# First-batch changes to a fused attention and maxout kernel: two weights loaded earlier, the v prefetch later, a z copy on ScalarE, more filler matmuls

## The chip, the cores and the metric

The kernel runs on one core of one Trainium2 chip. The metric is the device time of one execution in microseconds (us). Before the change it was 980.92 us, the median of three runs (979.39 to 981.77). All runs quoted here gave a correct result. Engines are named as in the profile: PE is TensorE's matmuls, PEld its weight loads, DVE is VectorE, ACT is ScalarE, POOL is GpSimd, SP is SyncE. POOL issues the software DMA queue here, SP the hardware one with all DMA transposes.

## The reference, cut to what matters

```python
batch, seq, d_model, d_qk = 8, 3072, 256, 64          # u, v: batch x seq x 256; z: batch x seq x 64
scores = (1.0 / S) * np.matmul(z, z.transpose(0, 2, 1))
attn = np.maximum(scores, 0.0) ** 2
x = u * np.matmul(attn, v)                             # then flattened to 24576 x 256
h1 = x @ w1                                            # w1, w2: 256 x 1024
h2 = x @ w2
out = np.maximum(h1, h2) @ w_out                       # w_out: 1024 x 256
```

The scores are symmetric in their two rows of z, and the kernel uses this: it computes a block of squared scores once and gets the mirrored block by a DMA transpose. It also uses max(h1, h2) = relu(h1 - h2) + h2, so it needs w1 - w2, and the product of w2 with w_out.

## The kernel before

A batch has 24 tiles of 128 rows, in 6 groups of 4 tiles. For each group the kernel forms products of all 24 tiles of attention with v in four PSUM accumulators (`attn_unit`), then empties ("drains") them, multiplies by u ("gate") and runs the two dense layers one group later. The first dense layers come after group 2, two groups at once. Everything that follows plays in the first three groups of batch 0, about the first 70 us.

Four parts matter. First, blocks of attention lie in 11 rotating buffers, and mirrors that are needed late are put off into a list:

```python
    apool = ctx.enter_context(tc.tile_pool(name="apool", bufs=11))
    ...
    def score_pair(b, g, m, dve_half=None, halves=False):
        blk = m // 2
        if m % 2 == 0:
            A[b, g, blk] = apool.tile([P, G, GW], bf16, name="a_sb")
        ...                                   # two score matmuls, ReLU of each half on ACT or DVE
        if not halves:
            nc.vector.tensor_mul(a[:, k : k + 2, :], r, r)
        if m % 2 == 1 and blk > g:
            if b == 0 and g < 2 and blk > 2:
                later.append((b, g, blk))
            else:
                mirror(b, g, blk)

    def mirror(b, g, blk):
        t = tpool.tile([P, G, G, P], bf16, name="at_sb")
        nc.sync.dma_start_transpose(...)      # reads A[b, g, blk], 0.5 MB
```

A new block whose buffer is still the source of a mirror must wait until that mirror has landed. Second, the loads of the weights, of the next u, of batch 1's z and of batch 1's v all go down one software queue, in program order:

```python
                if i + 1 < len(groups):
                    if i and n == 1:
                        load_u(*groups[i + 1])          # nc.gpsimd.dma_start
                    if n == 16:
                        turn_u(*groups[i + 1])          # nc.sync.dma_start_transpose
                if i == 1 and n == 6:
                    nc.vector.memset(w2_sb[:, 0, 0:1], 0.0)
                    for w_sb, w in ((w2_sb, moe_w2), (w1_sb, moe_w1), (w_out_sb, moe_w_out)):
                        nc.gpsimd.dma_start(
                            out=w_sb, in_=w.rearrange("(c p) f -> p c f", p=P)
                        )
                if later and n % 4 == 0 and (i > 1 or i == 1 and n > 12):
                    mirror(*later.pop(0))
                ...
                    if g == 2 and n == 10:
                        load_z(b + 1, 0, NT)
                    ...
                    if g >= 3 and n in (8, 14):
                        load_v(b + 1, (2 * (g - 3) + (n == 14)) * G, G)
```

The one-element memset makes the weight loads wait until DVE gets there. Each u has two natural-layout buffers (`unat`, bufs=2), so a load of u waits for the DMA transpose of the u two groups earlier, and what lies behind it in the queue waits too. Third, z is turned on PE at the start and copied out of PSUM by DVE or ACT:

```python
                if i == 0 and n == 5:
                    zT_pe(0, 12, 8, "dve")
                if i == 0 and n == 11:
                    zT_pe(0, 20, 4, "act")
```

Fourth, PE starts on dummy ("filler") matmuls, of which five lie between the first real pieces of work:

```python
        keep_warm([GW] * 5 + [P] * 2)
        ...
        zT_pe(0, 0, 4, "dve")
        keep_warm([P] * 5)
        ...
        ahead(1)
        zT_pe(0, 4, 8, "act")
        ahead(3)
```

`ahead(k)` computes score pairs up to number k. Of the first 22 pairs some have one ReLU half on DVE.

Of the kernel before, what the change touches and what calls it, by code (L numbers as in the profile page):

```python
# [11 lines left out]
def kernel(  # L12
# [10 lines left out]
    nc = tc.nc  # L23
    fp32 = mybir.dt.float32
# [8 lines left out]
    P = 128  # L33
    R = 64
    NT = S // P
    G = 4
    GW = G * P
    NG = NT // G
    KD = D // P
# [56 lines left out]
    def zT_pe(b, lo, n, engine):  # L96
        tp = mm_psum.tile([P, n, P], bf16, name="tpz", tag="mm")
        for j in range(n):
            nc.tensor.transpose(
                tp[:, j, :], zd[b][:, lo + j, :, :].rearrange("p h d -> p (h d)"), ident  # L100
            )
        copy = nc.scalar.copy if engine == "act" else nc.vector.tensor_copy
        copy(zT[b][:, lo : lo + n, :], tp)  # L103
# [18 lines left out]

    A = {}
    later = []

    def score_pair(b, g, m, dve_half=None, halves=False):
        blk = m // 2
# [142 lines left out]
    done = 0  # L270

    def ahead(upto):
        nonlocal done
        while done < min(upto, len(pairs)):
            early = done < 22
            score_pair(
                *pairs[done],
                dve_half=1 if early and (done % 2 == 0 or done < 2) else None,
                halves=done == 0,
            )  # L280
            done += 1
# [6 lines left out]
    with tc.manual_schedule():  # L288
        z32a = first_z(0, 4)
        z32b = first_z(4, 8)  # L290
        z32c = first_z(12, 12)
        warm = consts.tile([P, GW], bf16)
        nc.vector.memset(warm, 0.0)
        load_v(0, 0, G)
        make_identity(nc, ident)
        for g in range(1, NG):
            load_v(0, g * G, G)
        load_u(0, 0)
        load_u(0, 1)
        w1_sb = tpool.tile([P, KD, Dff], bf16, name="w1", tag="at_sb")  # L300
        w2_sb = tpool.tile([P, KD, Dff], bf16, name="w2", tag="at_sb")
        w2T_sb = tpool.tile([P, KD, KF, P], bf16, name="w2T", tag="at_sb")


        w_ps = mm_psum.tile([P, GW], fp32, name="warm_ps", tag="mm")

        def keep_warm(cols):
            for w in cols:
                nc.tensor.matmul(w_ps[:, :w], warm[:, :P], warm[:, :w], start=True, stop=True)

        keep_warm([GW] * 5 + [P] * 2)
        double_first(z32a, 0, 4)
        zT_pe(0, 0, 4, "dve")
        keep_warm([P] * 5)
        double_first(z32b, 4, 4)
        double_first(z32b, 8, 4, at=4)
        on_pool = (nc.gpsimd.tensor_copy, nc.gpsimd.tensor_copy)
        for c in range(0, 12, 4):
            double_first(z32c, 12 + c, 4, at=c, copies=on_pool)
        ahead(1)  # L320
        zT_pe(0, 4, 8, "act")
        ahead(3)

        waiting, sums = [], None
        for i, (b, g) in enumerate(groups):
            acc = [
                acc_psum.tile([P, KD, GW], fp32, name=f"acc{half}") for half in range(2)
            ]
            for n in range(NT):
                k = need[i, n]  # L330
                if b == 0 and g < 2:
                    ahead(max(k, done + 1) if n % 2 == 0 and n < 22 else k)
                else:
                    more = n in (0, 3, 6, 9, 12, 15, 18, 20)
                    ahead(max(k, min(done + 1, k + AHEAD)) if more else k)
                if i == 0 and n == 5:
                    zT_pe(0, 12, 8, "dve")
                if i == 0 and n == 11:
                    zT_pe(0, 20, 4, "act")
                attn_unit(b, g, n, acc, n == 0, n == NT - 1)  # L340
                if i and n == 12:
                    waiting.append((*groups[i - 1], gate(*groups[i - 1], sums)))
                if i == 0 and n == 14:
                    turn_u(0, 0)
                if i + 1 < len(groups):
                    if i and n == 1:
                        load_u(*groups[i + 1])
                    if n == 16:
                        turn_u(*groups[i + 1])
                if i == 1 and n == 6:  # L350

                    nc.vector.memset(w2_sb[:, 0, 0:1], 0.0)
                    for w_sb, w in ((w2_sb, moe_w2), (w1_sb, moe_w1), (w_out_sb, moe_w_out)):
                        nc.gpsimd.dma_start(
                            out=w_sb, in_=w.rearrange("(c p) f -> p c f", p=P)
                        )
                if later and n % 4 == 0 and (i > 1 or i == 1 and n > 12):
                    mirror(*later.pop(0))
                if i == 2 and n == 16:
                    nc.vector.tensor_sub(w15_sb, w1_sb, w2_sb)  # L360
                    for dc in range(KD):
                        tp = mm_psum.tile([P, KF, P], bf16, name="tpw", tag="mm")
                        for j in range(KF):
                            nc.tensor.transpose(
                                tp[:, j, :], w2_sb[:, dc, ts(j, P)], ident
                            )
                        nc.scalar.copy(w2T_sb[:, dc, :, :], tp)
                if b + 1 < B:
                    if g == 2 and n == 10:
                        load_z(b + 1, 0, NT)  # L370
                    if g == 3 and n == 4:
                        double_z(b + 1, 0, NT)
                        zT_dma(b + 1)
                    if g >= 3 and n in (8, 14):
                        load_v(b + 1, (2 * (g - 3) + (n == 14)) * G, G)
            if i == 2:
                for dc in range(KD):
                    ps = mm_psum.tile([P, D], fp32, name="w2o_ps", tag="mm")
                    for nb in range(KF):
                        nc.tensor.matmul(  # L380
                            ps,
                            w2T_sb[:, dc, nb, :],
                            w_out_sb[:, nb, :],
                            start=(nb == 0),
                            stop=(nb == KF - 1),
                        )
                    nc.scalar.copy(W2o_sb[:, dc, :], ps)

            now = waiting if i >= 2 else []
            g_sbs = [ff(w) for w in now[:1]]  # L390
            sums = drain(acc)
            for j, w in enumerate(now):
                if j:
                    g_sbs.append(ff(w))
                ff2(*w, g_sbs[j])
            if now:
                waiting = []
        w = (*groups[-1], gate(*groups[-1], sums))
        ff2(*w, ff(w), last=True)
# [29 lines left out]
```

## Time and profile before

| | value | where it is read |
|---|---|---|
| time, three runs | 980.92 us (979.39 to 981.77) | times |
| the execution that was profiled | 985.42 us, span 983.4 us, mean granted clock 0.996 | times, page |
| PE busy | 967.5 us, 98% of the span | part 1 of the page |
| PE waits for the gate of the dense layer (g_sb) | 4.6 us, once | waits of PE |
| clock from 62 to 66 us | 0.50 | busy time by stretch |

The page of the kernel before gives busy times (part 1) and the shares of the chain that ended last (part 4):

```profile
span 983.4 us, 19128 instructions
...
PE 967.5 (98%) x8036; PEld 517.9 (53%) x8036; DVE 497.4 (51%) x755; ACT 577.9 (59%) x1054; POOL 60.5 (6%) x118
...
PE 95%; DMA 3%; DVE 1%; ACT 0%; SPq 0%; issue 0%; DVEq 0%
```

PE bounds the kernel. The 3% of DMA in the chain is one transfer. The waits of PE in the kernel before (columns: who waited, for whom, total us, times, longest us):

```profile
PE d_ps L214 <- DVE g_sb L224: 4.6, 1, 4.6
PE acc_638 L183 <- DVE h_sb L194: 1.8, 1, 1.8
...
PE s_ps L135 <- DVE zT L103: 1.5, 1, 1.5
...
PE s_ps L135 <- ACT zT L103: 0.8, 1, 0.8
PE s_ps L135 <- DVE r_sb L146: 0.3, 1, 0.3
```

The waits of DVE in the kernel before, from 30 to 70 us, show why g_sb was late: DVE stood in its queue before a squaring whose destination buffer was still being read by a mirror transpose (at_sb).

```profile
DVE a_sb L154 <- DMA at_sb<-a_sb: 7.7, 1, 7.7
...
```

The tile at_sb of the kernel before in the trace, for issues from 28 to 66 us: the second line is its transit, shortest, median and longest, in us.

```profile
L164 SPq DMA_TRANSPOSE at_sb<-a_sb x6: 1920/2580/17570, 28.9 to 65.5; - x6
...
DMA to landing us min/median/max: 4.5/6.3/28.1
```

The 28.1 us one was issued at 32.80 and landed at 60.89. The busy time by stretch of the kernel before shows the stall and what follows it. After each stretch and its length come the busy us of PE, PEld, DVE, ACT and POOL (instructions in brackets), then the granted clock, the DMA share and GB/s:

```profile
58.00:60.00 2.00, 0.00 (x0) 0.00 (x0) 0.00 (x0) 0.38 (x1) 0.00 (x0) 1.00 1.62 36
60.00:62.00 2.00, 0.00 (x0) 0.00 (x0) 1.02 (x2) 0.00 (x0) 0.00 (x0) 0.71 1.23 239
62.00:64.00 2.00, 1.67 (x5) 0.57 (x5) 1.49 (x3) 0.00 (x0) 0.00 (x0) 0.50 1.15 221
64.00:66.00 2.00, 2.00 (x9) 1.14 (x8) 0.99 (x3) 1.56 (x3) 0.00 (x0) 0.50 1.12 211
66.00:68.00 2.00, 2.00 (x13) 1.47 (x12) 0.97 (x2) 0.00 (x0) 0.00 (x0) 0.58 1.14 210
```

PE does nothing for over four microseconds, and when it resumes the clock is at half, so that what it then does takes twice as long.

### The profile page before, as it was taken

How to read it: one execution, taken by the hardware profiler on the slowest of the kernel's cores; microseconds unless marked ns; L12 is line 12 of the kernel's file. 1: busy time of each engine (PE TensorE's matmuls, PEld its weight loads, DVE VectorE, ACT ScalarE, POOL GpSimd, SP SyncE). 2: the span in 40 equal slices, each digit the busy share in tenths (PEclk: the TensorE clock that was granted, in tenths of full speed). 3: DMA queues.
4: the chain of work that ended last, by engine and by line, in shares of the span. 5: the costliest groups of instructions: out<-in, count | busy, mean ns of one | idle time of the engine just before them, and what ended most of it. 6: DMA issues, size and time to landing. Idle time of an engine off the chain costs nothing.

```text
span 983.4 us, 19128 instructions
## 1 busy us (share of the span) xinstructions
PE 967.5 (98%) x8036; PEld 517.9 (53%) x8036; DVE 497.4 (51%) x755; ACT 577.9 (59%) x1054; POOL 60.5 (6%) x118
## 2 busy tenths in 40 slices
PE   8889999999999999999999999999999999999998
PEld 3455555555555555555555555555555555555555
DVE  6735545544454545455454554456535554355523
ACT  6745646664566646666466664666646665466623
POOL 3200000000010000000000000000000000000000
PEclk9989999999999999999999999999999999999999
DMA  9999958886498866977768875779747896576511
GB/s 183 127 174 212 183 104 160 163 163 133 92 164 163 156 120 119 163 156 153 119 123 166 164 147 109 144 152 166 146 106 145 162 163 119 117 138 134 96 55 43
DMA packets 346005, 137.69 MB, mean 140 GB/s; under 512 B 324544, under 2 KB 325696, under 8 KB 345920
## 3 DMA queue, kind: packets, MB, share of 16 engines
q1 hardware_dynamic: 329504, 106.98, 54.7%
q0 software_dynamic: 16416, 29.50, 19.8%
q8 instruction: 63, 1.03, 0.4%
q14 instruction: 22, 0.18, 0.1%
HBM read 59.77 MB, written 25.17 MB: 86 GB/s over the span
## 4 chain that ended last, share of the span: by engine, by line
PE 95%; DMA 3%; DVE 1%; ACT 0%; SPq 0%; issue 0%; DVEq 0%
PE d_ps L214 17%; PE o_ps L243 17%; PE s_ps L135 7%; PE o_ps L235 4%; DMA at_sb<-a_sb 3%; PE acc_12279 L183 1%; PE acc_12089 L183 1%; PE acc_4650 L183 1%; PE acc_4394 L183 1%; PE acc_4126 L183 1%; PE acc_2853 L183 1%; PE acc_2317 L183 1%; PE acc_2053 L183 1%; PE acc_1789 L183 1%; PE acc_11827 L183 1%; PE acc_11563 L183 1%
## 5 line engine op out<-in xcount | busy, mean ns | idle before, releaser
L150 ACT ACTIVATE r_sb<-s_ps 128x512 bf16<-128x512 f32 x660 | 358.7, 596 | 149.2 <-PE s_ps L135 149.1
L154 DVE TENSOR_TENSOR a_sb<-r_sb 128x1024 bf16<-128x1024 bf16 x335 | 231.5, 692 | 376.3 <-ACT r_sb L150 367.2
L183 PEld LDWEIGHTS <-v_sb 64*128 64x128 bf16 x4608 | 225.5, 94 | 269.8 <-issue 2.7
L243 PE MATMUL o_ps<-w_out_sb,g_sb 128*128 128x256 bf16 x1536 | 200.1, 273 | 0.0
L222 ACT ACTIVATE g_sb<-d_ps 128x512 bf16<-128x512 f32 x192 | 114.7, 598 | 115.5 <-PE d_ps L214 115.4
L224 DVE TENSOR_SCALAR g_sb<-d_ps 128x512 bf16<-128x512 f32 x192 | 132.7, 692 | 96.0 <-PE d_ps L214 96.0
L214 PE MATMUL d_ps<-xT,w_sb 128*128 128x512 bf16 x768 | 175.5, 382 | 4.6 <-DVE g_sb L224 4.6
L243 PEld LDWEIGHTS <-g_sb 128*128 128x128 bf16 x1536 | 150.8, 98 | 21.2
L250 ACT COPY o_sb<-o_ps 128x512 f32<-128x512 f32 x96 | 56.3, 586 | 130.8 <-PE o_ps L243 129.7
L135 PE MATMUL s_ps<-zT 64*128 64x512 bf16 x672 | 128.6, 378 | 2.6 <-DVE zT L103 1.5
L214 PEld LDWEIGHTS <-w_sb 128*128 128x128 bf16 x768 | 71.7, 98 | 103.9 <-issue 25.1
L113 POOL DMA_DIRECT2D un<-in_u_dram x48 | 25.7, 535 | 839.9 <-DMA uT<-un 818.7
L235 PE MATMUL o_ps<-W2o_sb,xT 128*128 128x256 bf16 x384 | 73.8, 274 | 0.0
L200 DVE SCALAR_TENSOR_TENSOR xT<-h_sb,uT 128x512 bf16<-128x512 f32 x96 | 61.8, 685 | 0.0
L135 PEld LDWEIGHTS <-zT 64*128 64x128 bf16 x672 | 32.9, 94 | 47.1 <-issue 9.9
L235 PEld LDWEIGHTS <-xT 128*128 128x128 bf16 x384 | 37.8, 98 | 14.5 <-issue 0.6
L109 POOL DMA_DIRECT2D v_sb<-in_v_dram x48 | 25.9, 548 | 0.8 <-POOLq L413 0.8
L183 PE MATMUL acc_203<-a_sb,v_sb 64*128 64x512 bf16 x48 | 12.5, 376 | 0.0
L183 PE MATMUL acc_202<-a_sb,v_sb 64*128 64x512 bf16 x48 | 12.5, 376 | 0.0
L183 PE MATMUL acc_1790<-a_sb,v_sb 64*128 64x512 bf16 x48 | 11.6, 376 | 0.0
L183 PE MATMUL acc_3331<-a_sb,v_sb 64*128 64x512 bf16 x48 | 11.6, 376 | 0.0
L183 PE MATMUL acc_4871<-a_sb,v_sb 64*128 64x512 bf16 x48 | 11.6, 376 | 0.0
(301 smaller groups left out, 1214.5 us busy)
## 6 DMA issues: line engine op xcount, KB each, us to landing
out_dram<-o_sb SPq DMA_DIRECT2D x47, 512.0 KB, 2.9
v_sb<-in_v_dram POOLq DMA_DIRECT2D x48, 256.0 KB, 7.1
un<-in_u_dram POOLq DMA_DIRECT2D x48, 256.0 KB, 5.0
zn<-in_z_dram POOLq DMA_DIRECT2D x7, 384.0 KB, 6.6
at_sb<-a_sb SPq DMA_TRANSPOSE x120, 4.4
uT<-un SPq DMA_TRANSPOSE x48, 3.6
w_132<-in_moe_w_dram POOLq DMA_DIRECT2D x1, 512.0 KB, 9.4
w_131<-in_moe_w_dram POOLq DMA_DIRECT2D x1, 512.0 KB, 11.9
```

The costliest lines, as they stand in the source:

```text
L109: nc.gpsimd.dma_start(out=v_sb[b][:, sl, :], in_=by_tile(v[b])[:, sl, :])
L135: nc.tensor.matmul(s_ps[h], zT[b][rows, 2 * m + h, :], zT[b][rows, ds(g * G, G), :].rearrange("p t c -> p (t c)"), start=True, stop=True,)
L150: nc.scalar.activation(r[:, h, :], s_ps[h], AF.Relu)
L154: nc.vector.tensor_mul(a[:, k : k + 2, :], r, r)
L183: nc.tensor.matmul(o, v_sb[b][rows, t, ts(dc, P)], mv, start=first, stop=last)
L200: nc.vector.scalar_tensor_tensor(out=xT[:, dc, :].rearrange("p (t r) -> p t r", r=P), in0=hs[dc].rearrange("p (t r) -> p t r", r=P), scala ...
L214: nc.tensor.matmul(d_ps, w15_sb[:, kc, ts(nb, P)], xT[:, kc, :], start=(kc == 0), stop=(kc == KD - 1),)
L222: nc.scalar.activation(g_sb[:, nb, :], d_ps, AF.Relu)
L224: nc.vector.tensor_single_scalar(out=g_sb[:, nb, :], in_=d_ps, scalar=0.0, op=ALU.max)
L235: nc.tensor.matmul(o_ps[:, t, :], xT[:, dc, ts(t0 + t, P)], W2o_sb[:, dc, :], start=(dc == 0), stop=False,)
L243: nc.tensor.matmul(o_ps[:, t, :], g_sb[:, nb, ts(t0 + t, P)], w_out_sb[:, nb, :], start=False, stop=(nb == KF - 1),)
L250: nc.scalar.copy(o_sb[:, t0 : t0 + 2, :], o_ps)
```

## The change

The intent: the DMA is almost empty from 26 to 30 us (4 GB/s), so w2 and w1 are loaded there, ahead of group 1, instead of together with everything else after 31 us. Batch 1's v comes later. The z copy that DVE started late goes to ACT, and DVE gets fewer ReLU halves (every third pair instead of every second). Six more filler matmuls go into the gaps of the start, and all fillers write into the accumulators, which are idle then, instead of a score buffer.

```diff
+    V_LATE = [(3, 14), (4, 8), (4, 14), (5, 2), (5, 8), (5, 14)]
...
-                dve_half=1 if early and (done % 2 == 0 or done < 2) else None,
+                dve_half=1 if early and (done % 3 == 0 or done < 2) else None,
...
-        w_ps = mm_psum.tile([P, GW], fp32, name="warm_ps", tag="mm")
...
+        first_acc = new_acc()          # the accumulators of group 0
...
-                nc.tensor.matmul(w_ps[:, :w], warm[:, :P], warm[:, :w], start=True, stop=True)
+                nc.tensor.matmul(
+                    first_acc[0][:, 0, :w], warm[:, :P], warm[:, :w], start=True, stop=True
+                )
...
         zT_pe(0, 4, 8, "act")
+        keep_warm([P] * 2)
+        ahead(2)
+        keep_warm([P] * 4)
         ahead(3)
...
-                    zT_pe(0, 12, 8, "dve")
+                    zT_pe(0, 12, 8, "act")
...
-                if i == 1 and n == 6:
-                    nc.vector.memset(w2_sb[:, 0, 0:1], 0.0)
-                    for w_sb, w in ((w2_sb, moe_w2), (w1_sb, moe_w1), (w_out_sb, moe_w_out)):
+                if (i, n) in ((0, 20), (1, 10)):
+                    w_in = ((w2_sb, moe_w2), (w1_sb, moe_w1)) if i == 0 else ((w_out_sb, moe_w_out),)
+                    nc.vector.memset(w_in[0][0][:, 0, 0:1], 0.0)
+                    for w_sb, w in w_in:
...
-                    if g >= 3 and n in (8, 14):
+                    if g >= 3 and n in (8, 14) and not late:          # late: batch 0
                         load_v(b + 1, (2 * (g - 3) + (n == 14)) * G, G)
+                    if late and (g, n) in V_LATE:
+                        load_v(1, V_LATE.index((g, n)) * G, G)
```

More of the change, by code (lines that the diff above doesn't have):

```diff
@@ L302, with new_acc @@
         w2T_sb = tpool.tile([P, KD, KF, P], bf16, name="w2T", tag="at_sb")
-        w_ps = mm_psum.tile([P, GW], fp32, name="warm_ps", tag="mm")
+        def new_acc():
+            return [
+                acc_psum.tile([P, KD, GW], fp32, name=f"acc{half}") for half in range(2)
+            ]
+        first_acc = new_acc()
         def keep_warm(cols):
             for w in cols:
-                nc.tensor.matmul(w_ps[:, :w], warm[:, :P], warm[:, :w], start=True, stop=True)
+                nc.tensor.matmul(
+                    first_acc[0][:, 0, :w], warm[:, :P], warm[:, :w], start=True, stop=True
+                )
         keep_warm([GW] * 5 + [P] * 2)
@@ L325 @@
         for i, (b, g) in enumerate(groups):
-            acc = [
-                acc_psum.tile([P, KD, GW], fp32, name=f"acc{half}") for half in range(2)
-            ]
+            acc = new_acc() if i else first_acc
             for n in range(NT):
@@ L368 @@
                 if b + 1 < B:
-                    if g == 2 and n == 10:
+                    late = int(b == 0)
+                    if (g, n) == (2, 10):
                         load_z(b + 1, 0, NT)
-                    if g == 3 and n == 4:
+                    if (g, n) == (3, 4):
                         double_z(b + 1, 0, NT)
                         zT_dma(b + 1)
-                    if g >= 3 and n in (8, 14):
+                    if g >= 3 and n in (8, 14) and not late:
                         load_v(b + 1, (2 * (g - 3) + (n == 14)) * G, G)
+                    if late and (g, n) in V_LATE:
+                        load_v(1, V_LATE.index((g, n)) * G, G)
             if i == 2:
```

## The prediction

> **What bounds the kernel.** TensorE: the page gives PE 967.5 us busy of 983.4 (98%), the chain that ended last is 95% PE, and in the stretches PE is 100% busy at clock 1.00 from 150 us almost to the end. So the change can earn only what is lost in the first 80 us (waits of PE, stretches):
>
> - 57.7 to 62.3 us: PE waits 4.6 us for DVE's g_sb. DVE had waited 7.7 us (53.3 to 60.9) for a mirror transpose whose source buffer the next A tile reuses. That transpose was issued at 32.8 and landed 28.1 us later (median 4.4). Meanwhile the software DMA queue carried w2, w1, w_out (1.5 MB as written), u, z, u and two v chunks; the last v landed at about 60.4, the transpose at 60.9.
> - 60.6 to 67.2 us: clock 0.5 after that idle time; 4.9 us of PE work at half speed, 2.4 us lost. The Trainium skill ("TensorE: Matmul & The Clock Gate", Part 1) says an idle array falls to half clock; this trace agrees (0.50 from 62 to 66).
> - 12.2 to 13.7: 1.5 us for a z copy on DVE, queued behind two squarings.
> - Two drain waits of 1.8 us, untouched; some 1.1 us of gaps before 8 us.
>
> **What the change does.** w2 and w1 (1 MB written) go out at about 22.4 us instead of 31.3. From 23 to 30 us the DMA is nearly empty (0 to 16 GB/s in 26 to 30); 1.25 MB with u takes an estimated 6 to 7.5 us at the 170 to 200 GB/s seen elsewhere: it fits. w_out stays at about 33 us; one v chunk instead of two follows u early. So about 1.6 MB of software traffic stands against the transposes after 33 us, instead of 2.9. "DMA: Bandwidth & Descriptors" (Issuing engines are not separate DMA queues) says all queues share the same engines; the 28 us transpose agrees.
>
> A catch from the built program: the A buffers are reused in another order. Group 3's first tile now waits for the first deferred mirror, its second for the second; before, only the second tile waited, for the first mirror. I estimate them to land at 35 to 46 and 46 to 50 us; they would stall PE after about 51 and 55. So no stall, with modest margin.
>
> The z copy on ScalarE costs 1.0 us instead of 0.68, but starts at once: TensorE goes on at about 12.7 instead of 13.7. Fewer ReLU halves on DVE (9 instead of 12 of the first 22): ScalarE stays under TensorE's 1.08 us a pair. The six extra fillers (53 to 107 ns each) fall into gaps: worth 0.
>
> **Sum.** 4.6 + 2.4 + 0.9 = about 8 us, all on the critical path; allowing for a remnant of the stall: 973.2 us, 970 to 978. Chances: faster by over 2% 0.01, within 2% 0.98, slower 0.01.
>
> **What would show it.** Right: no PE wait on g_sb near 57 us, clock 1.00 from 60 to 67, first deferred mirror landing within 15 us, w1 landed by 31 us, the PE wait on zT after 10 us below 0.7 us, group 3's first products at 70 to 71 us instead of 78.7. Wrong: DVE waiting for a mirror at 48 to 56 us, or a new PE wait between 60 and 140 us (batch 1's late v, mirrors of groups 3 and 4).
>
> **What would make it wrong.** The software backlog after 33 us still starving the second mirror: then 2 to 5 us of stall and the clock drop return, 976 to 980. More than 8 us would need the early ramp to shrink too.

## The result, and the profile after

The changed kernel took 977.98 us (median of 4 runs, 977.89 to 978.13). The kernel before, in the same rounds, took 981.35 us (4 runs, 979.39 to 982.09). The ratio is 0.9969, with a 95% interval of 0.9952 to 0.9986. Here and below a ratio is the mean time of one kernel's fast runs over that of the other's of the same rounds, so it is not quite the ratio of the medians that are quoted. All outputs are right. The change is a gain of 3.4 us (0.3%), within 2%. The prediction was 973.2 us, a gain of 7.7 us: less than half of it came, and 977.98 us lies at the upper edge of the predicted range.

The page of the kernel after:

```profile
span 975.8 us, 19097 instructions
...
PE 962.4 (99%) x7994; PEld 516.8 (53%) x8042; DVE 495.4 (51%) x752; ACT 580.3 (59%) x1058; POOL 61.0 (6%) x118
...
PE 98%; DVE 1%; issue 0%; ACT 0%
```

The DMA has left the chain. The waits of PE in the kernel after:

```profile
PE acc_431 L184 <- DVE h_sb L195: 1.8, 1, 1.8
...
PE s_ps L136 <- DVE r_sb L147: 1.5, 3, 0.7
...
PE s_ps L136 <- ACT zT L103: 0.6, 1, 0.6
PE s_ps L136 <- DVE zT L103: 0.2, 1, 0.2
```

There is no wait for g_sb. The wait for the z copy at 12 us fell from 1.5 us (on DVE) to 0.6 (now on ACT; the 0.2 us on DVE belongs to an earlier copy, at 4.5 us). The waits for r_sb, a ReLU half on DVE, grew from 0.3 to 1.5 us. But 1.0 us of these lies before 8 us, where the kernel before waited 0.8 us for ACT's zT and 0.3 for r_sb. New is the third, of 0.5 us, at 34.6 us (from PE's timeline: start, us busy, instruction, idle before it):

```profile
35.05 0.37 PE L136 MATMUL s_ps<-zT 64*128 64x512 bf16 x1 [0.47 <-DVE r_sb L147]
```

The waits of DVE in the kernel after, 30 to 70 us, hold no DMA:

```profile
DVE a_sb L155 <- ACT r_sb L151: 6.9, 9, 2.0
DVE g_sb L225 <- PE d_ps L215: 6.5, 8, 3.3
DVE h_sb L195 <- ACT h_sb L192: 0.7, 1, 0.7
```

The tile at_sb of the kernel after, issues from 28 to 66 us, and the busy time by stretch of the same places:

```profile
L165 SPq DMA_TRANSPOSE at_sb<-a_sb x10: 1901/2962/9177, 27.5 to 66.0; - x10
...
DMA to landing us min/median/max: 4.5/6.1/12.7
```

```profile
58.00:60.00 2.00, 2.00 (x17) 1.45 (x16) 1.83 (x3) 1.70 (x4) 0.00 (x0) 1.00 1.15 213
60.00:62.00 2.00, 2.00 (x20) 1.79 (x19) 0.79 (x2) 0.59 (x1) 0.00 (x0) 1.00 1.16 198
62.00:64.00 2.00, 1.95 (x15) 1.37 (x15) 0.00 (x0) 0.81 (x2) 0.00 (x0) 1.00 1.34 64
64.00:66.00 2.00, 2.00 (x11) 0.88 (x9) 1.60 (x3) 1.47 (x3) 0.00 (x0) 1.00 1.26 278
66.00:68.00 2.00, 2.00 (x18) 1.53 (x17) 1.17 (x2) 0.60 (x1) 0.00 (x0) 1.00 1.13 211
```

So in the profile nearly all of what was predicted came true. The first deferred mirror landed at 47.81 us and the second at 52.39, both later than estimated (35 to 46 and 46 to 50) but in time. w1 landed at 31.25 us ("by 31"). The clock is 1.00 from 60 to 67. The first products of group 3 start at 71.1 us ("70 to 71"). From one profiled execution to the other the time fell by 985.42 - 977.89 = 7.5 us, almost the predicted sum. The puzzle is that the medians fell by only 3.4 us.

To see where the 7.5 us lie, we marked in each trace the time at which the accumulators of groups 0, 1, 2 and 3 were drained (the end of DVE's last addition of that drain; in us):

```
                group 0   group 1   group 2   group 3
before            25.7      40.4      67.0      96.3
after             24.7      40.2      60.8      88.7
```

Group 0 ends 1.0 us earlier, and by the end of group 1 only 0.2 us of that is left. The stretch of group 2 is 26.6 us before (67.0 - 40.4) and 20.6 after: 6.0 us. The rest of the half clock falls into group 3: 29.3 us against 27.9, or 1.4 us. The sum is 0.2 + 6.0 + 1.4 = 7.6 us. After that the two traces run in parallel.

### The profile page after: what moved, and what is told of

Its sections match the earlier page's. It is cut to its first block, busy times and chain, and to the rows that moved or that the text cites. A ratio compares the mean times of both kernels' runs of the same rounds, so it can differ in the third digit from the quotient of the medians.

```text
span 975.8 us, 19097 instructions
## 1 busy us (share of the span) xinstructions
PE 962.4 (99%) x7994; PEld 516.8 (53%) x8042; DVE 495.4 (51%) x752; ACT 580.3 (59%) x1058; POOL 61.0 (6%) x118
## 3 DMA queue, kind: packets, MB, share of 16 engines
q1 hardware_dynamic: 329504, 106.98, 54.9%
q0 software_dynamic: 16416, 29.50, 19.4%
q8 instruction: 63, 1.03, 0.4%
## 4 chain that ended last, share of the span: by engine, by line
PE 98%; DVE 1%; issue 0%; ACT 0%
PE d_ps L215 17%; PE o_ps L244 17%; PE s_ps L136 8%; PE o_ps L236 4%; PE acc_12285 L184 1%; PE acc_12095 L184 1%; PE acc_10820 L184 1%; PE acc_10564 L184 1%; PE acc_10296 L184 1%; PE acc_10028 L184 1%; PE acc_9764 L184 1%; PE acc_9023 L184 1%; PE acc_8223 L184 1%; PE acc_7959 L184 1%; PE acc_1573 L184 1%; PE acc_11833 L184 1%
## 5 line engine op out<-in xcount | busy, mean ns | idle before, releaser
L215 PE MATMUL d_ps<-xT,w_sb 128*128 128x512 bf16 x720 | 171.4, 380 | 2.5
L136 PEld LDWEIGHTS <-zT 64*128 64x128 bf16 x672 | 33.1, 94 | 45.9 <-issue 10.0
L109 POOL DMA_DIRECT2D v_sb<-in_v_dram x48 | 25.9, 551 | 1.0 <-POOLq L426 0.8
```

The lines of the kernel that those rows point to most:

```text
L109: nc.gpsimd.dma_start(out=v_sb[b][:, sl, :], in_=by_tile(v[b])[:, sl, :])
L136: nc.tensor.matmul(s_ps[h], zT[b][rows, 2 * m + h, :], zT[b][rows, ds(g * G, G), :].rearrange("p t c -> p (t c)"), start=True, stop=True,)
L215: nc.tensor.matmul(d_ps, w15_sb[:, kc, ts(nb, P)], xT[:, kc, :], start=(kc == 0), stop=(kc == KD - 1),)
```

## The experiments

Three questions were open. Is the stall of the profiled execution (4.5 us longer than the median of the runs it was to explain, and 3.6 us longer than the slowest of them) typical of the kernel before? Which part of the change brings the 3.4 us? And where did the 0.9 us of the z copy go? The expectations below were put on record before each run; letters in them are working names of theories, which the sentences around them describe. The kernel before ran 11 times in each of six sets beside these kernels, on several chips. Its medians there were 980.86, 982.00, 981.77, 981.37, 980.79 and 979.85 us, 66 runs in all, from 977.94 to 987.25 us.

### The kernel before, profiled twice more (before_2, before_3)

No edit.

> The kernel before, unchanged, profiled a second time. The changed kernel's profiled run (977.89 us) equals its timed runs; the profiled run of before was 985.42 us against timed runs of 979.4 to 982.1. Theory A (draw): the stall at 53 to 67 us (late mirror, then half clock) differs from execution to execution, and the first profile caught a bad one. Then this profile shows a span of about 976.3 us plus whatever the PE wait on g_sb and the half-clock stretch cost in it: with a time of 979 to 982, a wait of 1 to 4 us, probably with no or a shorter clock drop; everything after 80 us takes the same time as in the first profile. Theory B (the stall is the same 4.6 + 2.4 us every time, and the timed runs are faster somewhere else, or profiling costs the old kernel 4 us): this profile again shows about 4.6 us of wait and the clock at 0.5, and a time near 985.

> The same, a third profile of before. Theory A: another length of the stall, again with time minus (PE wait on g_sb + half-clock loss) = about 978.4 us within 0.5. Theory B: as the first profile, 985.

Measured: 979.71 and 979.72 us, spans 977.7 and 977.8, clock 1.00. The waits of PE, and then of DVE (30 to 70 us), in before_2:

```profile
PE d_ps L214 <- DVE g_sb L224: 1.5, 1, 1.5
```

```profile
DVE a_sb L154 <- DMA at_sb<-a_sb: 4.6, 1, 4.6
```

The same mirror landed at 57.84 us instead of 60.89 (57.91 in before_3), PE waited 1.5 us instead of 4.6, and the clock stayed up, so that group 2 ended at 62.7 us instead of 67.0. These two executions lose 1.5 us where the first profile lost 4.6 + 2.4. So the stall is real in all three, but its size is a property of the execution, not of the kernel. DVE can absorb a part: 7.7 - 4.6 and 4.6 - 1.5 both leave 3.1 us, so in this order of the buffers a mirror that lands by about 56.3 us (57.84 less 1.5) costs PE nothing.

What holds the mirror up is the software burst. It landed just after the last v chunk in each of these: 60.41 then 60.89, 57.54 then 57.84, 57.53 then 57.91 us.

### One more buffer for attention blocks (one_more_buf)

```diff
-    apool = ctx.enter_context(tc.tile_pool(name="apool", bufs=11))
+    apool = ctx.enter_context(tc.tile_pool(name="apool", bufs=12))
```

This keeps the burst and takes away what made DVE wait for the mirror.

> The kernel before with 12 A buffers instead of 11, and nothing else: all DMA traffic stays as it was, but the second tile of group 3 no longer reuses the buffer that the first deferred mirror reads (it reuses one read by an earlier transpose; the tile after it now waits for that mirror, some 18 us later). Theory A (the stall is the whole difference, through that one wait): no PE wait on g_sb, no clock drop, and a time of about 978.4 to 978.9 us, within 1 us of the changed kernel, with its small scatter. Rival C (the DMA backlog itself costs the old kernel time, whatever waits for it): it stays near 981 and the stall moves to another wait.

Measured: 981.57 us (978.35 to 982.92, 6 runs), ratio 0.9998 [0.9977, 1.0019]: nothing gained. The wait for g_sb was gone, and a new one had come (waits of PE, 80 to 110 us; then the busy time by stretch):

```profile
PE s_ps L135 <- DMA zT<-zd: 2.5, 1, 2.5
```

```profile
92.00:96.00 4.00, 1.54 (x14) 0.50 (x12) 0.69 (x1) 0.95 (x2) 0.00 (x0) 0.90 1.23 258
96.00:100.00 4.00, 4.00 (x30) 1.47 (x26) 0.69 (x1) 2.17 (x4) 0.00 (x0) 0.68 1.23 150
```

Group 2 ended at 61.0 us, as in the changed kernel, but then PE reached batch 1 before batch 1's turned z had landed (95.37 us), and paid the wait and a clock drop there. The backlog of the DMA had moved on to the next consumer. In the changed kernel the same z landed at 86.43 us.

### The weight loads alone (weights_alone)

```diff
-                if i == 1 and n == 6:
-                    nc.vector.memset(w2_sb[:, 0, 0:1], 0.0)
-                    for w_sb, w in ((w2_sb, moe_w2), (w1_sb, moe_w1), (w_out_sb, moe_w_out)):
+                if (i, n) in ((0, 20), (1, 10)):
+                    w_in = ((w2_sb, moe_w2), (w1_sb, moe_w1)) if i == 0 else ((w_out_sb, moe_w_out),)
+                    nc.vector.memset(w_in[0][0][:, 0, 0:1], 0.0)
+                    for w_sb, w in w_in:
```

> The kernel before with only the weight loads moved (w2 and w1 at step 20 of group 0, w_out at step 10 of group 1); v, z copies and fillers as before. Theory D (two deadlines set by one DMA backlog between 31 and 95 us: the first deferred mirror, needed at about 53 us, and the transposed z of batch 1, needed at about 93 us; 1 MB less of software traffic after 31 us meets both): no PE wait on g_sb, none on batch 1's z, clock 1.00 throughout, z of batch 1 landing near 90 us; only the 0.9 us of the z copy at 12 us is missing, so 978.8 us (978.4 to 979.4), with a scatter under 1 us. Rival E (the later v loads are what removes the second wait): the wait on batch 1's z appears at about 93 us, 1 to 3 us long, and the time is 980 to 982 with the old scatter.

Measured: 980.86 us (978.09 to 985.61), ratio 1.0001 [0.9972, 1.003]. The headline of the change, on the kernel before, gains nothing. Its profiled execution (982.42 us) shows, in the waits of PE:

```profile
PE d_ps L214 <- DVE w_sb L361: 3.3, 1, 3.3
```

DVE again waited for mirrors, 8.4 us in two waits; they landed at 57.04 and 60.56 us. Two things worked against the move. The weights' earlier place shifts the reuse of the buffers, as the prediction had seen, so that an earlier block depends on the first deferred mirror: it now has to land by about 53.7 us to cost PE nothing (57.04 less 3.3), 2.6 us sooner than in the old order. And the freed room in the queue was filled at once by the next u and two chunks of v.

### Each DMA move taken back from the changed kernel (old_v, old_weights)

old_v puts back the old places of the v loads, old_weights the old place of the three weight loads. The diffs are the lines of the change above, reversed:

```diff
-                    if g >= 3 and n in (8, 14) and not late:
+                    if g >= 3 and n in (8, 14):
                         load_v(b + 1, (2 * (g - 3) + (n == 14)) * G, G)
-                    if late and (g, n) in V_LATE:
-                        load_v(1, V_LATE.index((g, n)) * G, G)
```

```diff
-                if (i, n) in ((0, 20), (1, 10)):
-                    w_in = ((w2_sb, moe_w2), (w1_sb, moe_w1)) if i == 0 else ((w_out_sb, moe_w_out),)
+                if i == 1 and n == 6:
+                    ...                       # w2, w1 and w_out together, as before
```

> The changed kernel with batch 1's v loads put back to the old places. Theory D: z of batch 1 lands 2 to 4 us later than the 86.4 us of the changed kernel, still before about 92, so nothing waits: 978.0 us, within 0.5 of the changed kernel. Rival E: a PE wait on batch 1's z of 1 to 3 us at about 92 us, and 979 to 981 us with a larger scatter.

> The changed kernel with the three weight loads put back together at step 6 of group 1; v stays late, z copies and fillers stay. Theory D: the first deferred mirror (which the second tile of group 3 waits for again) lands at about 53 to 58 us instead of 47.8, so DVE waits up to 4 us and PE 0 to 2 us at about 57; z of batch 1 lands at 88 to 93. Time 978 to 981 with a scatter of 1 to 4 us between runs. If only the v loads mattered (rival E), it equals the changed kernel at 978.0.

Measured: old_v 977.87 us (977.79 to 977.95), ratio 0.9966; old_weights 977.96 us (977.90 to 978.04), ratio 0.9967. Both are the changed kernel to 0.1 us. Neither move alone is needed, and the scatter that was expected of old_weights did not come. In old_weights the first mirror landed at 53.55 us and stalled nobody.

### Without the six new fillers (no_fill)

```diff
         zT_pe(0, 4, 8, "act")
-        keep_warm([P] * 2)
-        ahead(2)
-        keep_warm([P] * 4)
         ahead(3)
```

> The changed kernel without the six added filler matmuls (the one step of the second score pair before them goes too). The fillers stand in gaps in which TensorE waits for ScalarE and DVE anyway: 977.9 us, within 0.3 of the changed kernel. If they kept the clock up in the first 8 us (rival), it is slower by 0.5 to 2 us, with a clock under 1.00 or products of doubled length before 14 us.

Measured: 980.61 us (978.10 to 983.71), ratio 0.9995 [0.9971, 1.0018]. With both DMA moves and the z copy, but without six tiny matmuls that the prediction had priced at zero, the whole gain was gone. In the profiled execution (979.63 us) the mirror landed at 54.94 us, DVE waited 5.3 us for it and PE 1.4 (waits of DVE, 30 to 70 us):

```profile
DVE a_sb L155 <- DMA at_sb<-a_sb: 5.3, 1, 5.3
```

The trace shows what had changed in the DMA: u's transpose landed at 40.84 us instead of 44.55, so the next load of u went out at 41.37, before z (45.15) was through. It and v prolonged the burst to 54.72 us, and the mirror landed 0.2 us later. How could six matmuls do that? Three experiments follow.

### More instructions without filling a gap, and a filled gap without more instructions (count_only, same_count)

One theory was that only the position in PE's instruction stream matters. count_only is no_fill with the first warm-up block cut into more pieces of the same total; same_count is the changed kernel with fewer, bigger fillers, so that it has the instruction count of no_fill.

```diff
count_only, against no_fill:
-        keep_warm([GW] * 5 + [P] * 2)
+        keep_warm([GW] * 2 + [163] * 10 + [162])
same_count, against the changed kernel:
-        keep_warm([P] * 5)
+        keep_warm([214, 213, 213])
...
-        keep_warm([P] * 2)
+        keep_warm([2 * P])
         ahead(2)
-        keep_warm([P] * 4)
+        keep_warm([4 * P])
```

> The changed kernel without the six fillers in the gaps (as no_fill), but its first block of warm-up matmuls, 2816 columns in 7 matmuls, is cut into 13, still 2816 columns. So TensorE runs as many instructions as in the changed kernel, and the gaps stay empty. Theory F (the fillers matter only by their number: they move the point at which TensorE's next block[...] is fetched over the DMA, 32.9 us in the profiles of the changed kernel, old_v, and 33.6 in no_fill, past the issue of u's transpose for group 2; that decides whether this transpose lands before or after the burst of w_out, u and z, and so whether the next u and v lengthen the burst before the first deferred mirror is through): 978.0 us within 0.3, all runs within 0.5 of each other, fetch near 32.9, u's transpose landing at about 44.5, the mirror at 46 to 48. Theory G (the fillers keep TensorE's clock or pace by filling the gaps): as no_fill, 979 to 983 with a scatter of some us.

> The changed kernel with its gaps filled as before (256 and 512 columns), but in 2 matmuls instead of 6, and the five 128-column matmuls of the second warm-up block cut into 3 of the same sum. The gaps are as full as in the changed kernel, and TensorE runs exactly as many instructions as in no_fill. Theory F: as no_fill, 979 to 983 us with a scatter of 2 us or more between runs, the instruction fetch near 33.6 us, u's transpose landing at about 41, the mirror at about 55, DVE waiting for it. Theory G: as the changed kernel, 978.0 us with a scatter under 0.5.

Measured: count_only 978.25 us (977.85 to 979.95), ratio 0.9962, with two of six runs above 979.2 (979.40 and 979.95, both at clock 0.998). same_count 978.08 us (977.86 to 984.69), ratio 0.9967, five runs within 0.3 us and one at 984.69. Both gain, so neither theory stands as it was put. same_count speaks against the position in the instruction stream; count_only speaks against the filled gaps, since its gaps are open and its median is as good as that of the changed kernel. u's transpose landed at 44.42 and 45.56 us in the two profiles, late as in the changed kernel. What makes it land early in one kernel or execution and late in another was not found.

### Holding the next u back (gate_u)

```diff
 against no_fill, in load_u:
         un[b, g] = unat.tile([P, G, D], bf16, name="un")
+        if (b, g) == (0, 4):
+            nc.vector.memset(un[b, g][:, 0, 0:1], 0.0)
```

The one-element memset makes this load of u, and the v behind it, wait for DVE to get to group 3.

> no_fill with one thing more: the load of u for group 4, and the v chunk behind it in the same queue, is held back by a small write on VectorE until group 3 begins (about 71 us), whatever u's transpose for group 2 does. The burst then always ends with z at about 44 us. Theory F: the first deferred mirror lands by 48 us, DVE does not wait for a mirror, PE does not wait for g_sb or w_sb: 978.1 us within 0.4, scatter under 0.6 us, without any filler. If the backlog isn't what delays the mirror: as no_fill. A new wait on batch 1's z at about 92 us would show as 1 to 2 us.

Measured: 978.11 us (978.01 to 979.45), ratio 0.996. In the profile u's transpose landed early again, at 41.04 us, as in no_fill. Yet the mirror landed at 46.96 us, and there was no wait for it. Nothing but the u and v behind that transpose was held back. This shows the step of the mechanism that no_fill suggested: the loads let loose by u's transpose prolong the burst, and the mirror waits for the burst's end. (One of the six runs took 979.45 us at clock 0.998.)

### Where the z copy's gain went (z_on_dve, dve_to_20)

z_on_dve takes back the move of the z copy and of the ReLU halves. dve_to_20 ends the early ReLU halves on DVE one pair sooner, because of the changed kernel's wait of 0.5 us for r_sb at 34.6 us, where the ReLU half of pair 21 stood behind two gating products on DVE.

```diff
z_on_dve, against the changed kernel:
-                    zT_pe(0, 12, 8, "act")
+                    zT_pe(0, 12, 8, "dve")
...
-                dve_half=1 if early and (done % 3 == 0 or done < 2) else None,
+                dve_half=1 if early and (done % 2 == 0 or done < 2) else None,
dve_to_20, against the changed kernel:
-            early = done < 22
+            early = done < 21
```

> The changed kernel with the copy of z at step 5 of group 0 back on VectorE, and every second early pair sharing its ReLU with VectorE as before. By my prediction this part was worth 0.9 us: TensorE waits 1.5 us instead of 0.6 at 12 us, and everything after comes 0.9 us later: 978.9 us. It also moves the DMA issues by 0.9 us, so if the burst's order is a matter of chance it may fall into the slow pattern: then 980 to 983 with scatter.

> The changed kernel with the sharing of early ReLUs ended one pair earlier: pair 21, the last one, which falls on VectorE by the new rule (every third) but not by the old one (every second), goes to ScalarE whole. Theory H (the gain at 12 us is given back at 34 us, where this half stands behind the two gating products of group 0 on VectorE, and TensorE waits 0.7 us for its accumulator): no PE wait on the ReLU near 35 us, second drain ending at 39.4 us instead of 40.2, time 977.2 us (977.0 to 977.5). Rival (the gain is lost to something else between the two drains, or to the DMA): 978.0 us.

(The 0.7 us in the second text is the longest of the three waits for r_sb, which lies at 7.2 us; the one near 35 us is 0.5.)

Measured: z_on_dve 978.25 us (977.99 to 978.36), ratio 0.9958; dve_to_20 977.17 us (977.01 to 977.37), ratio 0.9963. With the copy on DVE PE waits 1.5 us for it and group 0 ends at 25.8 us instead of 24.7, but the median is only 0.27 us longer (978.25 - 977.98). With pair 21 moved off DVE the kernel is 0.81 us faster than the changed one (977.98 - 977.17), and group 1 ends at 39.3 us instead of 40.2; the wait near 35 us is gone (r_sb: 1.0 us in two waits, both before 8 us). So the 0.9 us were gained at 12 us and given back at 34 us. In the kernel before pair 21 (odd) had no half on DVE; with every third pair it had one.

### The fillers and the clock (gate_u_fill, gate_u_less)

gate_u still had one slow run in six, though its mirror came early. gate_u_fill is the changed kernel with the gate on u. gate_u_less is gate_u without the five fillers of the kernel before as well, which leaves larger gaps.

```diff
gate_u_fill, against the changed kernel: the two lines of gate_u
gate_u_less, against gate_u:
         zT_pe(0, 0, 4, "dve")
-        keep_warm([P] * 5)
```

> gate_u with the six fillers of the changed kernel. The stall cannot come (u for group 4 is held back), and the gaps are full. Theory I (slow runs of 1.3 to 2 us without a stall are TensorE running at half clock after gaps in the first 8 us; the fillers prevent that): all runs within 977.8 to 978.2 us, none slower. Rival (they come from elsewhere): one run or two of six at 979.3 or more, as in gate_u.

> gate_u with the five older fillers after the first transposes taken away too, so that the gaps in the first 8 us are larger. Theory I: more slow runs than in gate_u (one of six), at 979 to 981.5 us with a clock of 0.997 to 0.998, and the profile, if it catches one, shows products of double length (or a clock of 0.5) before 14 us. Rival: as gate_u.

Measured: gate_u_fill 978.11 us (977.80 to 978.41), ratio 0.9972, no slow run. gate_u_less 978.72 us (977.92 to 980.51), ratio 0.998 [0.9965, 0.9996], with three of six above 979.2. Its profiled execution (979.27 us) was one of the slow ones, and shows a cause: first PE's timeline (start, us busy, instruction, idle before it), then the busy time by stretch.

```profile
6.80 0.39 PE L138 MATMUL s_ps<-zT 64*128 64x512 bf16 x2 [0.69 <-DVE r_sb L149]
7.86 0.61 PE L138 MATMUL s_ps<-zT 64*128 64x512 bf16 x2 [0.67 <-DVE r_sb L149]
```

```profile
6.00:8.00 2.00, 0.64 (x5) 0.31 (x6) 1.85 (x5) 1.95 (x4) 0.39 (x2) 0.88 1.08 207
8.00:10.00 2.00, 2.00 (x12) 0.75 (x10) 2.00 (x3) 0.89 (x2) 2.00 (x4) 0.50 1.12 207
10.00:12.00 2.00, 2.00 (x18) 0.90 (x14) 1.21 (x3) 1.15 (x3) 1.30 (x3) 0.76 1.12 208
```

PE worked 0.64 of the 2 us from 6 to 8, and the clock fell to half from about 7.5 to 11.0 us (worked out from the three means of the clock). That it took some 3.4 us to come back agrees with the busy window that the Trainium skill gives ("TensorE: Matmul & The Clock Gate", Part 1). Group 0 ended at 26.1 us instead of 24.9 in gate_u: 1.2 us lost. gate_u_less lacks the five older fillers too, so this is not a measure of what the six new ones save.

The clock records in the traces place it. In gate_u_less full clock was first granted at 4.12 us and withdrawn at 7.54; in between PE was busy for 1.86 us, 0.64 of it transposes of z. In the changed kernel full clock was granted at 4.12 us as well, PE was busy for 2.52 us up to 7.54, 1.03 of it fillers, and the clock stayed up. But the gaps alone do not decide: gate_u's profile has the same two waits of 0.7 us and 0.72 us of work from 6 to 8, and no drop. There full clock had come at 5.42 us.

The scatter of all kernels goes with the fillers. "Slow" here means a run above 979.2 us, a line that was drawn after the runs:

```
gaps filled by the new fillers:
  after, old_v, old_weights, z_on_dve, dve_to_20, gate_u_fill,
  best, fill_alone, both_old_dma, same_count                       1 slow of 58 runs
gaps not filled:
  no_fill 5, count_only 2, gate_u 1, gate_u_less 3,
  weights_alone 4, one_more_buf 5, before_count 2                 22 slow of 42 runs
the kernel before                                                55 slow of 66 runs
```

Of the 22 slow runs, 14 belong to no_fill, weights_alone and one_more_buf, whose profiles show a wait for the mirror or for z. count_only and before_count have open gaps and a first warm-up block cut into 13, and only 4 slow runs of 12; why they scatter less than no_fill was not found.

count_only, gate_u and gate_u_less have no mirror stall in their profiles (of fast runs in the first two), and their slow runs end at 979.3 to 980.5 us, 1.2 to 2.5 us over the fast ones. The clock drop was seen in a profile only in gate_u_less; that the other slow runs of this kind are the same is argued from their times and mean clocks (0.998 in all but one), not shown.

The mean clocks also divide the scatter of the kernel before in part. A half-clock stretch of 3.4 us takes an estimated 0.0017 off the mean (half of 3.4 us in 978), so a run at 0.999 or 1.000 had none. Of the 55 slow runs 22 are such, up to 981.77 us: they lost their time in something else, such as the wait in before_2 and before_3. The other 33, at 0.998 or less, had a half-clock stretch; whether early or after a stall, the record does not say.

### The fillers alone, and both DMA moves taken back together (fill_alone, both_old_dma)

fill_alone is the kernel before with the six fillers (and all fillers in the accumulator), but its own loads and z copies. both_old_dma is the changed kernel with the edits of old_v and old_weights together.

```diff
fill_alone, against the kernel before:
-        w_ps = mm_psum.tile([P, GW], fp32, name="warm_ps", tag="mm")
...
+        first_acc = new_acc()
...
         zT_pe(0, 4, 8, "act")
+        keep_warm([P] * 2)
+        ahead(2)
+        keep_warm([P] * 4)
         ahead(3)
```

> The kernel before with only the six filler matmuls of after in the gaps of group 0; its loads, v prefetch and z copies stay as they were. If the fillers alone do it (they hold the clock and start the first drain about 0.9 us earlier, and the stall at group 3 does not come on its own), the median is 978.0 to 978.6 with a scatter under 1 us and no wait of PE for g_sb. If the late deferred mirror transpose is an own cause, the mirror lands at 57 us or later, VectorE waits 4 us or more for it, PE waits 1 to 3 us for g_sb or for w_sb, and the median is 979 to 981.

> The kernel after with both the two weight loads and the v prefetch at their old places; fillers and z copies on ScalarE stay. Each of the two moves was taken back alone without any cost (977.87 and 977.96). If the moves of DMA matter only together, the burst is that of the kernel before, the mirror lands at 57 us or later and the median is 979 to 981. If neither matters, the median is 977.8 to 978.2 and the first deferred mirror lands before 54 us.

Measured: fill_alone 978.55 us (978.16 to 979.13), ratio 0.9963 [0.9939, 0.9988]; both_old_dma 978.02 us (977.71 to 978.16), ratio 0.9957 [0.993, 0.9985]. So the fillers alone bring nearly all of the gain (fill_alone also moves all fillers into the accumulators, but no_fill has that too and gained nothing), and the two DMA moves, even together, bring none that the times show. The two differ by 0.5 us, and in the z copy and the ReLU halves alone. The waits of DVE in fill_alone, 30 to 70 us:

```profile
DVE a_sb L155 <- DMA at_sb<-a_sb: 3.1, 1, 3.1
```

The mirror landed at 56.45 us, DVE waited 3.1 us for it, and PE did not wait for g_sb at all: just the slack worked out above. In both_old_dma it landed at 54.75 us and DVE waited 1.5 us. The DMA moves do what they were meant to do, the mirror lands at 47.81 us with them; but in these executions there was nothing left to save.

Neither expectation fits in full. fill_alone's first drain did not come 0.9 us earlier (25.9 us against 25.7), because the z copy sets that time. And both_old_dma's mirror landed a little after the 54 us that were given.

### Six more instructions on the kernel before (before_count)

```diff
-        keep_warm([GW] * 5 + [P] * 2)
+        keep_warm([GW] * 2 + [163] * 10 + [162])
```

> The kernel before with its first warm-up block (2816 columns before any work) cut into 13 matmuls instead of 7: the same columns, six more instructions, no gap filled, all else as before. If six more TensorE instructions anywhere in the start are enough (as the 978.25 of count_only may mean), the median is 978.3 to 979.0 with at most two of six runs above 979.5. If it is the filled gaps between 6 and 12 us that steady the kernel, it is as scattered as the kernel before: median 980 to 982, three or more runs of six above 979.5.

Measured: 978.68 us (978.12 to 980.91), two of six above 979.5, beside a kernel before of 979.85 us (977.94 to 985.47); ratio 0.9987 [0.9961, 1.0014]. By its text the first expectation was met, but the interval holds 1, and in this set the kernel before was also at its best. The run is inconclusive. Its profile has the mirror landing at 54.83 us, after a last v chunk at 54.02, and no stall.

### A version that beats both (best)

The gate on u, pair 21 off DVE, and one thing more: the transposes of w2 for the product with w_out, which stood in group 2, go into PE's idle time while group 1 is drained.

```diff
 against the changed kernel, besides the edits of gate_u and dve_to_20
 (the lines that made these transposes in group 2, taken out, are not shown):
+            tps = []
+            if i == 1:
+                for dc in range(KD):
+                    tp = mm_psum.tile([P, KF, P], bf16, name="tpw", tag="mm")
+                    for j in range(KF):
+                        nc.tensor.transpose(tp[:, j, :], w2_sb[:, dc, ts(j, P)], ident)
+                    tps.append(tp)
             sums = drain(acc)
+            for dc, tp in enumerate(tps):
+                nc.scalar.copy(w2T_sb[:, dc, :, :], tp)
```

> The changed kernel with three things: u for group 4 held back (as gate_u_fill), pair 21 on ScalarE (as dve_to_20), and the 16 transposes of w2 (1.0 us of TensorE) moved from step 16 of group 2 into the drain of group 1, where TensorE waits 1.8 us. Expected: 0.7 us from the second, 1.0 from the third: 976.3 us (975.9 to 976.8), scatter under 0.6 us. A wait on batch 1's z at about 91 us would cost 1 us of it.

Measured: 976.06 us (975.99 to 976.21), ratio 0.9952 [0.9938, 0.9965]. The waits of PE:

```profile
PE acc L186 <- DVE h_sb L197: 2.5, 2, 1.8
```

The two drain waits are 2.5 us instead of 3.6. It is 1.9 us faster than the changed kernel (977.98 - 976.06), of which dve_to_20 accounts for 0.8. This is what the early weights are good for: they make the transposes of w2 possible at 39 us, where PE is idle; with w2 landing at 40.74 us, as in the first profile of the kernel before, they would have had to wait (argued, not run).

## Why the prediction was right or wrong

**Wrong: "Sum. 4.6 + 2.4 + 0.9 = about 8 us, all on the critical path."** The chain of causes was right for the execution in the profile, and the profiled times did fall by 7.5 us. But the sum was taken off the median of other executions. The profile was of a run of 985.42 us, and 980.92 us was the median to be predicted. The two further profiles of the kernel before lost 1.5 us to the stall and nothing to the clock after it, so that 4.6 + 2.4 = 7.0 us was 1.5 us there. And the DMA moves that were to earn it brought nothing that the times show (978.02 us with both taken back). Of the 66 timed runs, 13 took over 983.5 us; only such runs have room for a loss like that of the first profile. What an execution without it takes was there to be read: 985.42 - 7.0 = 978.4 us, close to what came. The fastest of the 66 took 977.94 us. No profile caught a run near the median, so what makes up the usual loss of some 3 us is known only in part. The changed kernel takes in every run what the kernel before takes in its best.

**Wrong: "The six extra fillers [...] worth 0."** Taken out, the median went back to 980.61 us; put alone into the kernel before, they gave 978.55 us. That they bring the gain is shown; how is shown only in part. With these six and the five older ones gone, the clock fell to half near 8 us in the one slow execution that was profiled, and cost 1.2 us. In the three profiles of the kernel before that drop did not occur, and 22 of its 55 slow runs lost no clock at all, so steadying the clock is not all that the fillers do. Whether they also keep the mirror early is open: in fill_alone's one profile it landed at 56.45 us, just at the limit.

**Wrong in place, right in mechanism: the 0.9 us of the z copy.** PE did go on sooner at 12 us (group 0 ended 1.0 us earlier). The prediction checked the load of ACT, but not that pair 21's ReLU half would now stand on DVE behind the gating products: a new wait of 0.5 us at 34.6 us, and 0.81 us gained when the half was moved off. Net, 0.27 us.

**Right: what the stall was.** PE waited for DVE, DVE for a mirror, the mirror for the software burst. one_more_buf cut the second link and the stall left; gate_u shortened the burst and the mirror came early. The prediction cited the Trainium skill, "DMA: Bandwidth & Descriptors", section "Issuing engines are not separate DMA queues", for the last link, and the runs agree: in nine profiles the mirror landed 0.2 to 0.8 us after the last software load, wherever that fell between 53.31 and 60.41 us. (weights_alone is the exception: its mirror landed at 57.04 us, before the v chunks at 57.61 and 58.90.) A way to see why it lands last: over the whole run the software queue moved 29.50 MB in 16416 packets, 1.8 KB each, and the hardware queue 106.98 MB in 329504, 0.3 KB each. The same page, section "SWDGE vs HWDGE vs iDMA", says that an engine takes turns between the two kinds of queue. If a turn is a packet, the transposes get an estimated 15% of the bytes while both are busy (325 bytes of every 325 + 1797). The trace of the kernel before has the share: from 47 to 57.5 us the hardware queue moved 0.37 of 1.82 MB, 20%, in 1458 packets against 809. So its share is small, as the estimate has it, but its turns are not one packet against one.

**Right: the catch of the buffer order,** and that the early weights fit into the gap. weights_alone shows both: w1 landed at 32.31 us, and the shifted reuse made PE wait 3.3 us at another place.

**Not seen: that an earlier weight load makes room for what queues behind it.** no_fill and weights_alone have 1 MB less after 31 us, and their mirrors still landed at 54.94 and 57.04 us, since the next u and v moved up.

**Open:** what decides when u's transpose lands (38.1 to 45.9 us in the profiles), and the cause of the one slow run with fillers, same_count's 984.69 us.

## What to carry to other kernels

Before a loss read from a profile is subtracted from a time, compare the profiled execution's own time with that time: here the profile was the bad execution, and its stall was not the median's. If a tuned kernel scatters by several microseconds while its fastest run is stable, ask first what the fast runs do not lose, for that is what a repair can gain. Price small fillers by a run and not by the gap that they fill: here six in gaps of under a microsecond cost nothing that the times show, and the kernel with them scattered far less. And a load that is moved earlier out of a full queue must be followed by a look at what moves up into its place.

## What the Trainium skill lacked or had wrong

- "TensorE: Matmul & The Clock Gate", Part 1 and "HAM oscillation — how this bites in real kernels": the pages give an idle window of about 3.4 us before the clock falls, and a rule of no idle gaps over that. Here gaps of at most 0.7 us each, with 1.86 us of work in the 3.4 us from 4.1 to 7.5 (0.64 of it transposes), brought 0.50 from 7.5 us (gate_u_less), and a single wait of 2.5 us brought a stretch mean of 0.68 (one_more_buf), while a single one of 1.5 us did nothing (before_2). The page's section "A second HAM failure mode: psum-queue depth-cycling" does name micro-idles; it lacks their size.
- "DMA: Bandwidth & Descriptors", "DMA Transpose (X-bar)" and "SWDGE vs HWDGE vs iDMA": there is no figure for a transpose against a full software queue. Here one of 0.5 MB took 28.1 us where the median of its kind was 4.4 us, and in nine profiles the first deferred one landed within 0.8 us of the last software load; from 47 to 57.5 us its queue got 20% of the bytes.
- No page that we read warns that a profile is one execution, and that it has to be set against the run times first: 985.42 us here against a median of 980.92.
